# Four late pairs of weight tiles staged in the two output tiles, and the opening written in another order, in a fused attention and feed-forward kernel

## The chip, the cores and the metric

The kernel runs on one core of a Trainium2 chip. The metric is the device time of one execution in microseconds (us), the median of several runs. TensorE (PE) multiplies, VectorE (DVE) and ScalarE (ACT) do the elementwise work, SyncE (SP) issues nearly all DMAs, GpSimd (POOL) only sets constants at the start.

## The reference

Two steps. For each of 8 batches and 8 heads, 512 tokens `x` (64 wide) and 32 states attend to each other in both directions; the results of a batch, 544 rows of 512, then go through a feed-forward network.

```python
scores = scale * np.matmul(x, state.transpose(0, 1, 3, 2))
a = np.exp(scores - scores.max(-1, keepdims=True))
a /= a.sum(-1, keepdims=True) + 1e-09
xread = np.matmul(a, state)                  # the tokens' rows: 512 a batch
scores2 = scale * np.matmul(state, x.transpose(0, 1, 3, 2))
...
sread = np.matmul(a2, x)                     # the states' rows: 32 a batch
...
h = x @ w_in                                 # 512 -> 2048, x now the 4352 rows
g = h * np.clip(h + 3.0, 0.0, 6.0) / 6.0
return (g @ w_out).astype(np.float32)        # 2048 -> 512
```

All of it is float32.

## The kernel before

**Products.** `xread` is never formed: `a @ state @ w_in` is computed as `a` times W' = `state @ w_in`, 256 rows of (head, state) by 2048 for each batch (`wprime`, products at L507, made for a chunk of 512 columns at a time, in the opening for smaller parts). A batch is 16 steps of 128 columns. `first(n)` multiplies `a` by one step of W' into a PSUM bank `ps_h` (there are two); ACT (L998) and DVE (L1000) make `g` of it; `second(n)` multiplies `g` by 128 rows of `w_out` into the four banks `acc0` to `acc3`, two steps later by rank. A float32 product is made of three products of rounded halves (L948): ACT writes the rounded `..._hi` (L305, L410) and DVE the rest `..._lo` (L306, L412). So a step has 6 first and 12 second products of 128x512. Step 0 of batch 0 alone is multiplied plainly (L977, L1017). A ninth pass has the 256 rows of `sread`.

**Attention.** The x of batch 0 is transposed by TensorE (L617), its scores (L682) go through a softmax in seven short DVE and ACT instructions for each quarter (L694 to L705), written into an output tile, and TensorE turns the result out of it (L713) into `a` (copies at L715 and L716). The x of every later batch is loaded in 16 small pieces (L494) into two `raw` tiles, which DVE transposes (four times L607); TensorE makes the scores (L507 on `tmp`). What `sread` needs is transposed by DVE (two times L871) and moved inside the memory by 16 small DMAs (L879); the x for it lies in `xb` (L478). TensorE reads it at L905.

**Weights.** Both matrices come in once. A load (L370) brings a tile of 128 rows, or a pair of such tiles; the words are put together by one ACT cast (L379) and one DVE instruction (L384) for each tile, a "decode" below; a tile of `w_out` is then split in halves (L410, L412). The dict `PLACES` says where a pair is staged: `early0` to `early3` are the rooms in which later halves of `w_out` will live, and the four rooms hold its ten pairs, one after the other. The other tiles of `w_out` go through the three `raw` tiles, which x and the moves of `sread` use as well.

**Output tiles.** The pool `outp` has two tiles, `ot`. One holds the softmax of batch 0 until it is turned; later they hold the results of a batch (`L1041`, `L1044`, stored at L1052) and every third W' chunk.

**What sets the order.** Every operation is put into a plan (`Plan.add`) with its engine, a cost, a rank, what it reads and writes. `Plan.order` makes one sequence: as long as the list `OPENING` lasts, it takes the operation whose number stands there, after that the one that could start first by the costs and ranks. Each engine executes its part of the sequence in order, SP's DMAs among them; a DMA waits in SP's queue until the tile that it fills is free. Between TensorE's operations of the opening, `issue` puts filler products on a constant (`wake`, L1235), as many as the plan's times leave room for.

Of the kernel before, what the change touches and what calls it, by code (L numbers as in the profile page):

```python
# [12 lines left out]
U32 = mybir.dt.uint32  # L13
# [53 lines left out]
class Plan:  # L67
# [33 lines left out]
    def order(self):  # L101
# [19 lines left out]
        channel = 0.0  # L121
        flying = [0.0] * 8
        row, self.start, self.took = [], [0.0] * n_ops, [0.0] * n_ops
        while len(row) < n_ops:
            best = None
            told = opening[len(row)] if len(row) < len(opening) else None
            for e, numbers in open_ops.items():
# [3 lines left out]
                for n in numbers:  # L131
# [6 lines left out]
                    t = max(clock[e], ready[n])  # L138
# [30 lines left out]
            if size:  # L169
                channel = max(channel, t + 0.5) + size / self.transfer  # L170
                done = max(channel, t) + 2.0
                flying.remove(min(flying))
                flying.append(done)
# [33 lines left out]
def tile_state_attention_then_hardswish_ffn(  # L207
# [82 lines left out]
    def Q(rank, size, do, reads=(), writes=(), after=()):  # L290
        return plan.add("Q", 0.49, rank, do, reads, writes, after, size)
# [46 lines left out]
    def weight(kind, k, n, place, rank, load_rank):  # L338
# [8 lines left out]
        def pieces():  # L347
            if place[0] == "raw":
                return get(place, lambda: stage.tile([P, 512, 2], U32, name="raw")).unsqueeze(1)
            c, half = HOMES[int(place[0][-1])]  # L350
            t = get(place, lambda: cpool.tile(
                [P, 2, 512, 2], U32, name=place[0], tag=f"w_out_{half}{c}"))
            return t[:, place[2] : place[2] + n] if n == 1 else t
# [34 lines left out]
        Q(load_rank, {("in", 1): 537.0, ("in", 2): 925.0, ("out", 1): 465.0, ("out", 2): 930.0}[kind, n], load, writes=[key])  # L388
        lo = key + ("lo",)
        wide = 0.08 + 0.54 * n  # L390
        for i in range(n):
            top = ("top", (kind, k + i))
            S_(0.62, rank, lambda i=i: upper(i), [key], [top])
# [31 lines left out]
    wp_at, scores_at = {}, {}  # L425

    def load_state(b, rank, after=()):
# [15 lines left out]
        if b < TURNED:  # L443
            plan.add("Q", 1.35, rank, load, (), [key], after, 400.0)
            return
        plan.add("Q", 1.8, rank, load_blocks, (), [key], after, 400.0)
# [36 lines left out]
    def load_turned(b, rank, after=()):  # L483


        for g in range(NG):
            key = ("raw", ("x", b, g))
            for i in range(2):
                for u in range(2):
                    for k in range(D // NS):  # L490
# [9 lines left out]
                        Q(rank, 65.536, load, writes=[(*key, i, u, k)], after=after)  # L500
# [163 lines left out]
    def tokens_by_rows(after, banks):  # L664
# [9 lines left out]
        for q in range(NQ):  # L674
# [3 lines left out]
            def scores(q=q, ps=ps):  # L678
# [17 lines left out]
            V(0.35, r[1], lambda m1=m1, view=view, bt=bt: nc.vector.tensor_tensor(  # L696
                bt(), view(), wide(m1()), op=ALU.subtract), [m1_key, ps], [part_key])
            S_(0.38, r[2], lambda bt=bt: nc.scalar.activation(bt(), bt(), AF.Exp, scale=SCALE),
# [567 lines left out]
```

## Time and profile before

| | us |
|---|---|
| median of 3 runs | 657.22 (656.95 to 658.18) |
| the profiled execution | 655.46 |
| its span | 653.7 |
| TensorE busy in it | 641.6 |
| granted TensorE clock | 0.999 |
| DMA, moved in it | 46.25 MB |

A line of the table of stretches has the stretch in us from the span's start, its length, then busy us (and instructions) of PE, PE's weight loads, DVE, ACT and POOL, the granted clock, the DMA engines' busy share and GB/s. A line in order of time has start, duration, engine, line, operation, the tile written and the tiles read, and sizes; x2 means two such instructions in a row, and in brackets stands how long the engine had been idle before it and what ended that. `SPq` lines are issues of DMAs; the data lands some us later.

### The profile page before, as it was taken

What the parts mean: (1) busy time and instruction counts of PE and PEld (TensorE: products, weight loads), DVE (VectorE), ACT (ScalarE), POOL (GpSimd) and SP (SyncE); (2) the same over time, 40 slices, a digit from 0 to 9 for tenths busy, and PEclk for the clock granted to TensorE, in tenths of its full rate; (3) what the DMA queues carried; (4) which work ended last, traced back from release to release, by engine and by line L of the source; (5) the groups of instructions that cost most, each with busy time, mean ns of one, the idle gap of its engine ahead of it and who ended that gap; (6) DMA issues with size and microseconds to landing.
All of it is one profiled execution on the core that took longest, in us unless ns stands there. A gap on an engine that the chain in (4) does not pass through costs nothing.

```text
span 653.7 us, 9891 instructions
## 1 busy us (share of the span) xinstructions
PE 641.6 (98%) x3934; PEld 500.3 (77%) x3934; DVE 393.0 (60%) x685; ACT 293.1 (45%) x510; POOL 1.2 (0%) x7
## 2 busy tenths in 40 slices
PE   8999999989999999999999999999999999999997
PEld 6577778767877877787868777787778787788896
DVE  6988785468487356944686356834595344443552
ACT  5988454334344343633344344534344333433542
POOL 0000000000000000000000000000000000000000
PEclk9999999999999999999999999999999999999999
DMA  8985500604840503132131405041131001000101
GB/s 285 339 268 179 117 10 10 118 15 107 120 133 11 86 2 103 33 51 46 64 70 20 78 1 134 1 76 21 66 66 30 3 1 66 0 1 2 64 1 33
DMA packets 135270, 46.25 MB, mean 71 GB/s; under 512 B 123576, under 2 KB 129208, under 8 KB 135096
## 3 DMA queue, kind: packets, MB, share of 16 engines
q1 hardware_dynamic: 135080, 45.36, 28.5%
q8 instruction: 31, 0.51, 0.3%
q10 hardware_dynamic: 144, 0.26, 0.1%
q14 instruction: 15, 0.12, 0.1%
HBM read 33.02 MB, written 8.91 MB: 64 GB/s over the span
## 4 chain that ended last, share of the span: by engine, by line
PE 85%; SPq 4%; DMA 4%; DVE 3%; ACT 2%; issue 1%; DVEq 0%; ACTq 0%
PE acc L948 51%; PE ps_h L948 27%; PE ps_s L507 4%; PE ps_h L507 2%; SPq L879 1%; SPq L494 1%; DMA raw<-in_x_dram 1%; DMA early<-in_moe_w_out_dram 1%; PE ps_h L905 1%; SPq L478 1%; ACT tops L379 1%; DMA early<-in_moe_w_in_dram 1%; DMA raw<-raw 1%; DVE w_in L384 0%; ACT g L998 0%
## 5 line engine op out<-in xcount | busy, mean ns | idle before, releaser
L948 PE MATMUL acc<-w_out_hi,g_hi 128*128 128x512 f32 x540 | 213.4, 395 | 0.1
L948 PE MATMUL acc<-w_out_lo,g_hi 128*128 128x512 f32 x540 | 210.6, 390 | 0.0
L948 PE MATMUL acc<-w_out_hi,g_lo 128*128 128x512 f32 x540 | 210.2, 389 | 0.0
L998 ACT ACTIVATE g<-ps_h,three 128x512 f32<-128x512 f32 (+1 forms) x144 | 95.6, 664 | 221.9 <-PE ps_h L948 210.9
L1000 DVE SCALAR_TENSOR_TENSOR g<-g,ps_h 128x512 f32<-128x512 f32 (+1 forms) x144 | 94.3, 657 | 150.7 <-ACT g L998 149.9
L948 PEld LDWEIGHTS acc<-w_out_hi,g_hi 128*128 128x128 f32 x540 | 101.4, 188 | 34.5 <-issue 12.6
L306 DVE TENSOR_TENSOR g_lo<-g,g_hi 128x512 fp32r<-128x512 f32 (+1 forms) x143 | 93.9, 657 | 49.2 <-ACT g_hi L305 48.0
L305 ACT CAST g_hi<-g 128x512 fp32r<-128x512 f32 (+1 forms) x143 | 85.0, 595 | 85.1 <-DVE g L1000 80.3
L948 PEld LDWEIGHTS acc<-w_out_hi,g_lo 128*128 128x128 f32 x540 | 101.4, 188 | 21.7 <-DVE g_lo L306 0.2
L948 PEld LDWEIGHTS acc<-w_out_lo,g_hi 128*128 128x128 f32 x540 | 101.5, 188 | 19.6
L948 PE MATMUL ps_h<-aT_hi,wp_hi 128*128 128x512 f32 (+1 forms) x246 | 90.4, 367 | 3.3 <-DVE wp_lo L306 2.9
L948 PE MATMUL ps_h<-aT_hi,wp_lo 128*128 128x512 f32 (+1 forms) x246 | 89.1, 362 | 0.4 <-DVE wp_lo L306 0.4
L948 PE MATMUL ps_h<-aT_lo,wp_hi 128*128 128x512 f32 (+1 forms) x246 | 89.1, 362 | 0.0
L948 PEld LDWEIGHTS ps_h<-aT_hi,wp_hi 128*128 128x128 f32 x246 | 46.4, 189 | 13.4 <-issue 3.6
L948 PEld LDWEIGHTS ps_h<-aT_lo,wp_hi 128*128 128x128 f32 x246 | 46.4, 189 | 8.2 <-DVE aT_lo L306 0.5
L948 PEld LDWEIGHTS ps_h<-aT_hi,wp_lo 128*128 128x128 f32 x246 | 46.4, 189 | 7.8 <-DVE wp_lo L306 0.7
L948 PE MATMUL ps_h<-aT_hi,wp 128*128 128x512 f32 x144 | 50.2, 389 | 0.0
L948 PEld LDWEIGHTS ps_h<-aT_hi,wp 128*128 128x128 f32 x144 | 27.0, 188 | 5.7
L607 DVE STREAM_TRANSPOSE tmp<-raw 128x512 f32<-128x512 f32 x28 | 19.1, 699 | 15.9 <-DMA raw<-in_x_dram 12.3
L948 PE MATMUL ps_h<-aT_lo,wp 128*128 128x512 f32 x72 | 28.0, 389 | 0.0
L379 ACT CAST tops<-early 128x512 f16<-128x512 bf16 x25 | 18.2, 779 | 5.0 <-DMA early<-in_moe_w_out_dram 2.8
L507 PE MATMUL ps_s<-w_in,stT 64*32 64x512 f32 (+1 forms) x320 | 19.6, 548 | 0.0
(124 smaller groups left out, 427.4 us busy)
## 6 DMA issues: line engine op xcount, KB each, us to landing
xb<-in_x_dram SPq DMA_DIRECT2D x32, 256.0 KB, 4.2
out_dram<-ot SPq DMA_DIRECT2D x8, 1024.0 KB, 4.4
raw<-in_x_dram SPq DMA_DIRECT2D x112, 64.0 KB, 2.1
early<-in_moe_w_in_dram SPq DMA_DIRECT2D x7, 1023.0 KB, 5.8
early<-in_moe_w_out_dram SPq DMA_DIRECT2D x4, 1023.5 KB, 5.4
raw<-raw SPq DMA_DIRECT2D x112, 32.0 KB, 2.0
raw<-in_moe_w_out_dram SPq DMA_DIRECT2D x7, 511.8 KB, 7.1
early<-in_moe_w_in_dram SPq DMA_DIRECT2D x2, 511.0 KB, 6.4
```

Of the source, the lines that this page charges most:

```text
L305: S_(cost, rank, lambda: nc.scalar.copy(hi(), src()), reads, [writes[0]])
L306: V(cost, rank, lambda: nc.vector.tensor_tensor(lo(), src(), hi().bitcast(F32), op=ALU.subtract), [*reads, writes[0]], [writes[1]])
L379: nc.scalar.copy(out[..., 1], digits(pieces().bitcast(BF16), 2, i))
L478: nc.sync.dma_start(x_tile(b)[:, :, k, :], x_v[b, k])
L494: nc.sync.dma_start(t[rows, i].rearrange("t (a c) -> t a c", c=NS), x[b, 4 * g + 2 * i + u, :, k * NS : (k + 1) * NS].rearrange("(a t) c - ...
L507: nc.tensor.matmul(out[u][cols, :], made["stT", b][rows, cols], moving(q)[rows], start=True, stop=True,)
L607: V(0.7, rank[0], lambda q=q, key=key: nc.vector.transpose(xT(b, q), made[key][:, q % 2]), [(*key, q % 2, u, k) for u in range(2) for k in ...
L879: nc.sync.dma_start(dst[:, :, q], src[:, :, c])
L905: nc.tensor.matmul(bank(pr)[cols, u * D : (u + 1) * D], e2T(b, u)[:, j * P + q * NS : j * P + (q + 1) * NS], x_tile(b)[:, NG * q + u, j, : ...
L948: nc.tensor.matmul(ps, l, r, start=start and k == 0, stop=stop and k == n - 1)
L998: S_(cost + 0.05, rank, lambda: nc.scalar.activation(g(), bank(ps)[:, :width], AF.Relu, bias=three), [ps], [g_key])
L1000: V(cost, rank, lambda: nc.vector.scalar_tensor_tensor(g(), g(), 6.0, bank(ps)[:, :width], op0=ALU.min, op1=ALU.mult), [ps], [g_key])
```

## The change

Four pairs are staged elsewhere: `w_out` 4-5, 6-7 and `w_in` 12-13, 14-15 go into the two output tiles (under the tile name `wide`), two pairs in each, one after the other, in place of `early2` and `early3`. In the plan their loads come after the first multiplications of batch 0's softmax. `OPENING` is written anew and has 675 numbers for 631. Some costs in the plan are other numbers: they have no effect but through the order.

```diff
-5 2 1 0 24 3 4 35 11 80 36 27 6 29 30 28 93 31 32 33 14 49 34 41 25 19 50 51 37 26 52 42 38 39 53 43 57 54 44
+5 0 1 3 11 2 4 33 24 80 34 27 93 29 31 32 6 30 28 37 19 41 38 12 14 57 42 43 35 44 58 39 36 59 45 60 13 49 40
...
-                channel = max(channel, t + 0.5) + size / self.transfer
-                done = max(channel, t) + 2.0
+                channel = max(channel, t + 1.3) + size / self.transfer
+                done = channel + 1.6
...
-    def Q(rank, size, do, reads=(), writes=(), after=()):
-        return plan.add("Q", 0.49, rank, do, reads, writes, after, size)
+    def Q(rank, size, do, reads=(), writes=(), after=(), cost=0.53):
+        return plan.add("Q", cost, rank, do, reads, writes, after, size)
...
+            if place[0] == "ot":
+                return get(place, lambda: outp.tile([P, 2, 512, 2], U32, name="wide", tag="ot"))
...
+          after=first_exps if place[0] == 'ot' else ())
...
-            S_(0.62, rank, lambda i=i: upper(i), [key], [top])
+            S_(0.65, rank, lambda i=i: upper(i), [key], [top])
...
-        plan.add("Q", 1.8, rank, load_blocks, (), [key], after, 400.0)
+        plan.add("Q", 2.6, rank, load_blocks, (), [key], after, 400.0)
...
-            V(0.35, r[1], lambda m1=m1, view=view, bt=bt: nc.vector.tensor_tensor(
+            shifted = V(0.35, r[1], lambda m1=m1, view=view, bt=bt: nc.vector.tensor_tensor(
                 bt(), view(), wide(m1()), op=ALU.subtract), [m1_key, ps], [part_key])
+            first_exps.append(shifted)
...
-        ("in", 4): ("early0", 1), ("in", 6): ("early1", 1), ("out", 4): ("early2", 1),
-        ("out", 6): ("early3", 1), ("in", 8): ("early2", 2), ("in", 10): ("early3", 2),
-        ("out", 8): ("early2", 3), ("out", 10): ("early3", 3), ("in", 12): ("early2", 4),
-        ("in", 14): ("early3", 4),
+        ("in", 4): ("early0", 1), ("in", 6): ("early1", 1), ("out", 4): ("ot", ("w", 0)),
+        ("out", 6): ("ot", ("w", 1)), ("in", 8): ("early2", 2), ("in", 10): ("early3", 2),
+        ("out", 8): ("early2", 3), ("out", 10): ("early3", 3), ("in", 12): ("ot", ("w", 2)),
+        ("in", 14): ("ot", ("w", 3)),
```

The other edits of the diff are costs of the same kind. In the changed kernel the lines stand up to 7 further down. Three places show what the new list moves.

The first is DVE at the end of batch 0's softmax (`ot`, with sums `s`) up to the first `g`; `early` and `raw` rows are decodes, `nm` belongs to the states' softmax. Before:

```order
L384 SCALAR_TENSOR_TENSOR raw<-raw,tops 128x512
L702 TENSOR_SCALAR s_190<-s_190 128x8
L704 RECIPROCAL s_190<-s_190 128x8 x2
L705 TENSOR_TENSOR ot<-ot,s_190 128x8x32 x2
L781 TENSOR_REDUCE nm_297<-ps_s 128x2
L384 SCALAR_TENSOR_TENSOR w_in_179<-early_142,tops 128x4x128 x2
L716 COPY w_in_314<-acc_308 128x512
L781 TENSOR_REDUCE nm_297<-ps_s 128x2
L306 TENSOR_TENSOR wp_lo<-acc_253,wp_hi 128x128
```

and now:

```order
L711 TENSOR_TENSOR ot<-ot,s_190 128x8x32 x2
L307 TENSOR_TENSOR wp_lo<-acc_275,wp_hi 128x128
L387 SCALAR_TENSOR_TENSOR w_in_240<-early_137,tops 128x4x128
L307 TENSOR_TENSOR wp_lo<-acc_274,wp_hi 128x128
L722 COPY w_in_309<-acc_304 128x512
L387 SCALAR_TENSOR_TENSOR w_in_240<-early_137,tops 128x4x128
L307 TENSOR_TENSOR aT_lo<-w_in_309,aT_hi 128x512 x2
L387 SCALAR_TENSOR_TENSOR raw<-raw,tops 128x512
L787 TENSOR_REDUCE nm_346<-ps_s 128x2
L1006 SCALAR_TENSOR_TENSOR g<-g,ps_h 128x512
```

Both `wp_lo` stand ahead of the copy of `a`, one decode fewer stands ahead of the last multiplications, and the first reduction for the states stands behind `aT_lo`.

The second is SP's queue of loads from about 30 us on (the pieces `raw<-in_x_dram` are x of batch 1). Before:

```order
L370 DMA early_444<-in_moe_w_out_dram 128x2x2047
L370 DMA raw<-in_moe_w_out_dram 128x2047
L370 DMA early_497<-in_moe_w_out_dram 128x2x2047
L440 DMA st_raw<-in_state_dram 32x4x32 x4
L370 DMA raw<-in_moe_w_out_dram 128x2047
L370 DMA early_562<-in_moe_w_in_dram 128x4x1023
L370 DMA early_595<-in_moe_w_in_dram 128x4x1023
L370 DMA early_641<-in_moe_w_out_dram 128x2x2047
L370 DMA early_683<-in_moe_w_out_dram 128x2x2047
L494 DMA raw<-in_x_dram 32x16x32 x16
```

and now, from the load of `w_in` 6-7 on:

```order
L373 DMA early_327<-in_moe_w_in_dram 128x4x1023
L373 DMA wide<-in_moe_w_out_dram 128x2x2047 x2
L373 DMA early_429<-in_moe_w_in_dram 128x4x1023
L499 DMA raw<-in_x_dram 32x16x32
L373 DMA early_496<-in_moe_w_out_dram 128x2x2047
L499 DMA raw<-in_x_dram 32x16x32 x7
L373 DMA raw<-in_moe_w_out_dram 128x2047
L499 DMA raw<-in_x_dram 32x16x32 x3
L373 DMA wide<-in_moe_w_in_dram 128x4x1023
L445 DMA st_raw<-in_state_dram 32x4x32 x4
L499 DMA raw<-in_x_dram 32x16x32 x2
L373 DMA early_646<-in_moe_w_out_dram 128x2x2047
```

After these come one piece of x, the last `wide` pair (`w_in` 14-15), the last two pieces and the last three tiles of `w_out`. The two `w_out` pairs have moved ahead of `w_in` 10-11, and x of batch 1 lies between the weights.

The third is DVE ahead of the scores of batch 2 (the rows `tmp<-raw` transpose its x). Before:

```order
L306 TENSOR_TENSOR wp_lo<-ps_s,wp_hi 128x512
L306 TENSOR_TENSOR wp_lo<-ps_h,wp_hi 128x512
L1000 SCALAR_TENSOR_TENSOR g<-g,ps_h 128x512
L306 TENSOR_TENSOR g_lo<-g,g_hi 128x512
L306 TENSOR_TENSOR wp_lo<-ps_s,wp_hi 128x512
L1000 SCALAR_TENSOR_TENSOR g<-g,ps_h 128x512
L607 STREAM_TRANSPOSE tmp<-raw 128x512 x2
L306 TENSOR_TENSOR wp_lo<-ps_h,wp_hi 128x512
L306 TENSOR_TENSOR g_lo<-g,g_hi 128x512
```

and now:

```order
L307 TENSOR_TENSOR wp_lo<-ps_h,wp_hi 128x512
L307 TENSOR_TENSOR g_lo<-g,g_hi 128x512
L307 TENSOR_TENSOR wp_lo<-ps_s,wp_hi 128x512
L307 TENSOR_TENSOR wp_lo<-ps_h,wp_hi 128x512
L307 TENSOR_TENSOR wp_lo<-ps_s,wp_hi 128x512
L1006 SCALAR_TENSOR_TENSOR g<-g,ps_h 128x512
L456 STREAM_TRANSPOSE stT<-st_raw 128x128
L1006 SCALAR_TENSOR_TENSOR g<-g,ps_h 128x512
L307 TENSOR_TENSOR g_lo<-g,g_hi 128x512
L612 STREAM_TRANSPOSE tmp<-raw 128x512 x4
```

All four `wp_lo` (the last W' products of batch 1) now stand ahead of the four transposes.

More of the change, by code (lines that the diff above doesn't have):

```diff
@@ L386, in join @@
             )
-        Q(load_rank, {("in", 1): 537.0, ("in", 2): 925.0, ("out", 1): 465.0, ("out", 2): 930.0}[kind, n], load, writes=[key])
+        Q(load_rank, {("in", 1): 537.0, ("in", 2): 960.0, ("out", 1): 465.0, ("out", 2): 1000.0}[kind, n], load, writes=[key],
+          after=first_exps if place[0] == 'ot' else ())
         lo = key + ("lo",)
@@ L425, in tile_state_attention_then_hardswish_ffn @@
     wp_at, scores_at = {}, {}
+    first_exps = []
     def load_state(b, rank, after=()):
@@ L443, in load_state @@
         if b < TURNED:
-            plan.add("Q", 1.35, rank, load, (), [key], after, 400.0)
+            plan.add("Q", 1.39, rank, load, (), [key], after, 400.0)
             return
-        plan.add("Q", 1.8, rank, load_blocks, (), [key], after, 400.0)
+        plan.add("Q", 2.6, rank, load_blocks, (), [key], after, 400.0)
     def turn_state(b, rank, after):
@@ L499, in load @@
                             )
-                        Q(rank, 65.536, load, writes=[(*key, i, u, k)], after=after)
+                        Q(rank, 65.536, load, writes=[(*key, i, u, k)], after=after, cost=0.62)
     def all_heads(b, out, moving):
@@ L795, in exps @@
                                              accum_out=r2()[:, NG + NG * i + u : NG + NG * i + u + 1])
-                    S_(0.6, rank(5), exps, [ps[i], n_key], [("tmp", ("e2", b, u), i), (*r_key, u, i)])
+                    S_(0.48, rank(5), exps, [ps[i], n_key], [("tmp", ("e2", b, u), i), (*r_key, u, i)])
             V(0.08, rank(6), lambda: nc.vector.scalar_tensor_tensor(
@@ L865, in move @@
                             nc.sync.dma_start(dst[:, :, q], src[:, :, c])
-                        Q(rank, 16.384, move, [blocks_key], [e2T_key(b, g, c, q)])
+                        Q(rank, 16.384, move, [blocks_key], [e2T_key(b, g, c, q)], cost=0.65)
             return
@@ L879, in move @@
                     nc.sync.dma_start(dst[:, :, q], src[:, :, c])
-                Q(rank, 32.768, move, [(*blocks_key, g) for g in range(NG)], [e2T_key(b, 0, c, q)])
+                Q(rank, 32.768, move, [(*blocks_key, g) for g in range(NG)], [e2T_key(b, 0, c, q)], cost=0.65)
     def put(c, ps, cols):
```

45 rows, old and new, of the table OPENING are left out of this document.

## The prediction

> **What bounds the kernel now.** I read the page's busy shares first, then the table of stretches (busy us of each engine, its instructions, granted clock, DMA share, GB/s), then TensorE's own order of time, looking for starts further apart than the work between them. The last line is from the chain of waits: the twelve second products of one step take 2.72, so one product 0.227 and the six first ones of a step 1.36.
>
> ```profile
> PE 641.6 (98%) x3934; PEld 500.3 (77%) x3934; DVE 393.0 (60%) x685; ACT 293.1 (45%) x510; POOL 1.2 (0%) x7
> 0.00:20.00 20.00, 16.49 (x166) 12.38 (x166) 13.51 (x39) 13.28 (x27) 1.17 (x7) 1.00 0.88 304
> 20.00:60.00 40.00, 39.20 (x235) 25.32 (x234) 34.83 (x63) 35.12 (x67) 0.00 (x0) 1.00 0.84 285
> 60.00:120.00 60.00, 60.00 (x377) 45.47 (x376) 43.32 (x76) 31.01 (x53) 0.00 (x0) 1.00 0.24 45
> 120.00:140.00 20.00, 17.08 (x147) 13.02 (x145) 10.05 (x16) 5.10 (x8) 0.00 (x0) 1.00 0.47 86
> 200.00:600.00 400.00, 400.00 (x2340) 314.83 (x2340) 224.06 (x369) 161.01 (x269) 0.00 (x0) 1.00 0.20 42
> ...
> 204.52 2.72 PE acc L948 x12
> ```
>
> TensorE ends the kernel. From 200 to 600 us it is busy for 400.00 of 400.00, so nothing is to be had there. What an order can win lies before 200: the time until the first real product, and the places where TensorE waits. In 20 to 60 ACT and DVE are busy for 35 of 40 us each: there the covers are thin.
>
> ```profile
> 132.13 0.39 PE L948 MATMUL acc<-w_out_lo,g_hi 128*128 128x512 f32 x1
> 132.35 0.39 PE L948 MATMUL acc<-w_out_hi,g_lo 128*128 128x512 f32 x1
> 135.66 0.47 PE L948 MATMUL ps_h<-aT_hi,wp_hi 128*128 128x512 f32 x1 [2.92 <-DVE wp_lo L306]
> 132.91 0.71 DVE L607 STREAM_TRANSPOSE tmp<-raw 128x512 f32<-128x512 f32 x1 [2.74 <-DMA raw<-in_x_dram]
> 134.23 0.71 DVE L607 STREAM_TRANSPOSE tmp<-raw 128x512 f32<-128x512 f32 x1 [0.61 <-DMA raw<-in_x_dram]
> 134.86 0.65 DVE L306 TENSOR_TENSOR wp_lo<-ps_h,wp_hi 128x512 fp32r<-128x512 f32 x1
> ```
>
> The largest wait: a product starts 0.23 us after its neighbour (132.13, 132.35), and the next one 3.31 after that. TensorE wants wp_lo; DVE has it behind two transposes of batch 2's x, and these wait for x. The wait is made by DVE's order: the transposes aren't needed until the scores of batch 2, at 138.
>
> **The change part by part.**
>
> ```profile
> 168.35 0.39 PE L948 MATMUL acc<-w_out_lo,g_hi 128*128 128x512 f32 x1
> ```
>
> It adds no product, cast, decode or byte. It takes 8 of 43 fillers out of the opening, and from this row on (the last 2,477 of TensorE's) the sequence on every engine is the old one. So the gain is what TensorE has won by this row, and what it waits less behind it.
>
> *Opening, to the second products of step 0* (L1017, now L1023).
>
> ```profile
> 16.83 0.74 DVE L705 TENSOR_TENSOR ot<-ot,s 128x256 f32<-128x256 f32 x2
> 17.63 1.09 PE L713 MATMUL acc<-ident,ot 128*128 128x128 f32 x8 [0.56 <-DVE ot L705]
> 18.56 1.15 PE L1235 MATMUL ps_h<-wake 128*128 128x256 bf16 x9
> 19.29 0.68 DVE L716 COPY w_in<-acc 128x512 f32<-128x512 f32 x1
> 19.54 1.88 PE L977 MATMUL ps_h<-w_in,tmp 128*128 128x512 f32 x4
> 22.37 0.50 PE L948 MATMUL ps_h<-aT_hi,wp_lo 128*128 128x512 f32 x1 [0.37 <-DVE wp_lo L306]
> 22.83 0.68 DVE L1000 SCALAR_TENSOR_TENSOR g<-g,ps_h 128x512 f32<-128x512 f32 x1
> 23.57 2.07 PE L1017 MATMUL acc<-raw,g 128*128 128x512 f32 x4
> ```
>
> DVE's softmax of batch 0 had four weight decodes (0.68) in it and has three. A full decode is 0.6 at DVE's pace (two take 1.28); I count 0.4, since the first score arrives a little later. The last multiply then ends at 17.15 for 17.57. TensorE's turn follows: 1.09, plus 0.2 to its reader, 18.45. DVE has wp_lo, a decode and wp_lo in that pause (1.2), then in a row, as the new order has them: the copy, a decode, two aT_lo, a decode, one reduction, the multiply that makes g: six by 0.6 and 0.68, to 22.75. TensorE has 5 fillers for 9 after the turn (9 took 0.98, so 0.44 less); step 0 then starts near 18.75, and step 1 is through by 22.2, as both wp_lo are early now and the wait at 22.37 goes. The second products so wait for g, and start at 22.8 for 23.57: **-0.8**. Bounds: +0.3, if none of the decode's time is won and g comes later still; -1.4, if they start as soon as TensorE is free at 22.2.
>
> [...]
>
> *Late weight pairs in the output tiles.*
>
> ```profile
> 30.52 0.37 SPq L370 DMA_DIRECT2D early<-in_moe_w_out_dram  x1
> 34.65 0.37 SPq L370 DMA_DIRECT2D early<-in_moe_w_out_dram  x1
> 37.48 1.43 ACT L379 CAST tops<-early 128x512 f16<-128x512 bf16 x2 [2.04 <-DMA early<-in_moe_w_out_dram]
> 44.03 0.39 PE L948 MATMUL acc<-w_out_hi,g_lo 128*128 128x512 f32 x1
> 44.82 0.50 PE L948 MATMUL ps_h<-aT_hi,wp_hi 128*128 128x512 f32 x1 [0.40 <-DVE g L1000]
> ```
>
> The pairs w_out 4-5 and 6-7 were asked for at 30.52 and 34.65, when the early tiles came free; ACT stood 2.04 for the first, DVE's multiply came late behind it, and TensorE lost 0.79 - 0.23 = 0.56. Now one output tile is free from the start and the other after the turn (18.45), so both loads are issued near 20, behind three w_in pairs.
>
> ```profile
> 10.00:20.00 10.00, 8.80 (x119) 6.57 (x119) 9.93 (x31) 8.99 (x19) 0.00 (x0) 1.00 1.04 390
> ```
>
> In the first 20 us DMA moves 304 x 20 = 6.1 MB. The loads ahead of these five pairs are 5.3 MB; of the pairs' 5.2 MB 0.8 are then in too, and 4.4 take 11.3 us at 390 GB/s: the last is in near 32. ACT has 23 entries between the aT_hi casts (done near 20) and its first cast of a wide tile, 0.52 each (35.12 in 67): near 32 too, when w_out 4-5 has been in for 2.7, and the next two casts follow six entries later. So ACT's wait goes: **-0.6**. Bounds: 0 (ACT and DVE are full there) and -0.6.
>
> *x of batch 1 earlier.*
>
> ```profile
> 65.04 8.29 SPq L494 DMA_DIRECT2D raw<-in_x_dram  x16
> 76.16 2.12 PE L507 MATMUL ps_s<-tmp,stT 64*32 64x512 f32 x16
> 76.45 0.71 DVE L607 STREAM_TRANSPOSE tmp<-raw 128x512 f32<-128x512 f32 x1 [1.55 <-DMA raw<-in_x_dram]
> 138.01 1.09 PE L507 MATMUL ps_s<-tmp,stT 64*32 64x512 f32 x16
> ```
>
> The scores of batch 1 take 2.12 where those of batch 2 take 1.09: they wait for the last transpose. SP's 16 issues of x now stand between the weights, 14 of them ahead of the last w_in pair. That pair waits for the lo half of w_out 6-7, 47 DVE entries behind the g of step 0 (22.75); at 40 us for 63 entries this is near 52, so x is in by 56. TensorE reaches the scores near 68: from 22.8 on 4.0 for step 0's second products, ten steps of first products (1.36), eight of second ones (2.72), six W' sets and the turn of e2 with their switches (6). **-1.0**, bounds 0 and -1.0.
>
> *x of batch 2 behind wp_lo.*
>
> ```profile
> 107.48 0.69 DVE L871 STREAM_TRANSPOSE raw<-tmp 128x512 f32<-128x512 f32 x1
> 108.23 0.76 SPq L879 DMA_DIRECT2D raw<-raw  x1
> 109.19 2.15 SPq L440 DMA_DIRECT2D st_raw<-in_state_dram  x4
> 131.98 0.60 SPq L494 DMA_DIRECT2D raw<-in_x_dram  x1
> ```
>
> All four wp_lo now precede the four transposes, so the 3.31 - 0.23 go: **-3.1**. What is late next? The moves (L879) can't start before the second L871, and with x and xb the queue needs 23.75 us from 108.23 to its last issue; DVE is through with x at 134.9, 26.7 after 108.23. The four state loads (2.15) now go ahead of the moves, so I take 24.5. From the second L871 (L877) to the scores TensorE has seven steps of first products, 6.25 of second ones and two W' sets: 9.5 + 17.0 + 2.1 = 28.6. So x is transposed some 3 us before the scores. Behind the transposes DVE has the multiply g of step 24, needed only after the scores: covered by 2.2 us of scores and reading. Bounds: -3.1, and -0.5 if the queue runs as slowly as in 146 to 176, when 16 moves and 16 pieces shared it with an output store.
>
> *Behind 168.4.*
>
> ```profile
> 179.46 0.39 PE L948 MATMUL acc<-w_out_hi,g_lo 128*128 128x512 f32 x1
> 179.97 0.50 PE L948 MATMUL acc<-w_out_hi,g_hi 128*128 128x512 f32 x1
> ```
>
> 0.51 - 0.23: 0.28 lost, as DVE stood for batch 3's x. Its pieces are issued with the earlier moves now: **-0.3**, bounds 0 and -0.3.
>
> *At nothing*: plan numbers that reach no row behind 168.4; the tile name, which changes no byte; out of batch 0 still stored behind the moves, before batch 1 wants its tile. Without that cover the output multiplies would wait for the store.
>
> *New small waits*: the row order cannot show them, the trace of before does not have them. The old order, written by the same kind of plan, left 0.56 and 0.28 besides its two large ones; I give the new one **+1.0**, bounds 0 and +3 (one wait like the largest).
>
> Sum: -0.8 - 0.6 - 1.0 - 3.1 - 0.3 + 1.0 = -4.8. The profiled execution took 655.46 (span 653.7): 650.7. The median of the runs is 657.22, 1.8 above it; the forecast for the median is **652.4**.
>
> **The rivals.**
>
> *All goes and nothing new comes*: -5.8, with a faster opening -6.4: about 651. For: every term has its own row. Against: DVE and ACT full in 20 to 60.
>
> *x of batch 2 is late still*: the wait moves from wp_lo to the scores. For: 36 issues in one queue, each near 0.6. Against: 3 us of cover. At the term's bound, 2.6 less gain: 655.0.
>
> [...]
>
> *Nothing won*: DVE and ACT are the bound from 20 to 100, and early loads only wait in their tiles; the large wait is paid in several small ones. 657.2. Against: DVE idles for 17 of 60 us in 60 to 120.
>
> *Slower*: two pairs in one tile. w_in 14-15 cannot be asked for before w_out 6-7 has left the output tile (near 52, above), and W' of chunk 3 wants it near 64, 4 before the scores. From issue to decode an early pair took 37.48 - 30.52 + 1.9, near 9 us; so 3 us of cover. It decides once that pair is over 3 us late; 8 us late costs 5, and as all steps of chunk 3 queue behind it on an ACT that is full, 2 more: 657.22 - 4.8 + 7 = 659.4. For: x pieces now lie among these loads. Against: DMA is 0.73 to 0.77 busy in 40 to 60, as this shows.
>
> ```profile
> 40.00:50.00 10.00, 9.60 (x59) 7.08 (x58) 8.37 (x13) 9.01 (x16) 0.00 (x0) 1.00 0.77 238
> 50.00:60.00 10.00, 9.97 (x67) 6.38 (x67) 8.18 (x15) 8.76 (x16) 0.00 (x0) 1.00 0.73 257
> ```
>
> **How the numbers follow.** Forecast 0.49 (651.3 to 653.8), all goes 0.11, x late 0.18, cold array 0.03, nothing won 0.09, slower 0.10. A measurement of this kernel can tell 0.2%, 1.3 us, from no change. Faster by more (under 655.9): 0.49 + 0.11 + 0.18 + 0.03 = 0.81; same 0.09; slower 0.10. The range that leaves out 2 in 10 runs from 650.6 to 655.7.
>
> **What would show it.** In the changed kernel: L983 starts near 18.8 and L1023 near 22.8; no ACT cast of a wide tile waits for a DMA; the scores of batch 1 last 1.1; no wait for wp_lo over 0.5 us; the scores of batch 2 start near 130; TensorE is 5 us earlier at the row that was at 168.4. The prediction is wrong if a wait of over 2 us stands anywhere between 20 and 168, or if the opening is no earlier.

## The result, and the profile after

| us | before | after |
|---|---|---|
| median, runs | 657.64 (4) | **648.87** (4: 648.32 to 649.16) |
| the profiled execution, its span | 655.46, 653.7 | 649.16, 647.3 |
| TensorE busy in it | 641.6 | 639.0 |

The ratio is 0.9868 (95% interval 0.9851 to 0.9885): 1.3% faster, below the forecast's 652.4 and below the low end of its range, 650.6. The two profiled executions lie 6.3 apart, the two medians 8.8: this difference is the first thing to be explained.

From the changed kernel's page, its busy shares:

```profile
PE 639.0 (99%) x3926; PEld 500.9 (77%) x3926; DVE 393.3 (61%) x685; ACT 292.4 (45%) x510; POOL 1.2 (0%) x7
```

Its table of stretches, with the columns as before:

```profile
20.00:60.00 40.00, 39.27 (x232) 27.88 (x231) 35.58 (x63) 32.92 (x62) 0.00 (x0) 1.00 0.96 290
60.00:120.00 60.00, 59.58 (x389) 44.58 (x388) 45.09 (x77) 33.38 (x58) 0.00 (x0) 1.00 0.26 59
120.00:140.00 20.00, 20.00 (x161) 15.76 (x160) 14.45 (x28) 7.79 (x14) 0.00 (x0) 1.00 0.26 34
200.00:600.00 400.00, 400.00 (x2346) 315.05 (x2346) 220.29 (x364) 160.41 (x268) 0.00 (x0) 1.00 0.20 42
```

From 120 to 140 us TensorE is busy throughout, where it was for 17.08. From 200 to 600 it is busy for 400.00 of 400.00, as before. Its order of time on TensorE at the places that the prediction named:

```profile
16.75 1.09 PE L719 MATMUL acc<-ident,ot 128*128 128x128 f32 x8 [0.22 <-DVE ot L711]
18.22 1.88 PE L983 MATMUL ps_h<-w_in,tmp 128*128 128x512 f32 x4
22.22 3.87 PE L1023 MATMUL acc<-raw,g 128*128 128x512 f32 x8 [0.73 <-DVE g L1006]
61.34 0.39 PE L954 MATMUL acc<-w_out_hi,g_lo 128*128 128x512 f32 x1
62.15 0.50 PE L954 MATMUL ps_h<-aT_hi,wp_hi 128*128 128x512 f32 x1 [0.42 <-DVE g L1006]
68.41 1.09 PE L512 MATMUL ps_s<-tmp,stT 64*32 64x512 f32 x16
128.71 1.09 PE L512 MATMUL ps_s<-tmp,stT 64*32 64x512 f32 x16
177.40 1.09 PE L512 MATMUL ps_s<-tmp,stT 64*32 64x512 f32 x16
```

The row of the kernel before that stands at the place of the last one:

```profile
183.75 1.09 PE L507 MATMUL ps_s<-tmp,stT 64*32 64x512 f32 x16
```

The second products of step 0 start 1.35 earlier (22.22 for 23.57). The scores of batch 1 last 1.09, for 2.12. Those of batch 2 start at 128.71 with nothing waiting. One new wait is there: 62.15 - 61.34 - 0.23 = 0.58. At the scores of batch 3, where TensorE's order is the old one again, it is 6.35 earlier, and the spans differ by 6.4: all that this pair of executions shows was won before.

### The profile page after: what moved, and what is told of

It reads as the page before. It is cut to its first block, busy times and chain, and to the rows that moved or that the text cites. A ratio compares the mean times of both kernels' runs of the same rounds, so it can differ in the third digit from the quotient of the medians.

```text
span 647.3 us, 9869 instructions
## 1 busy us (share of the span) xinstructions
PE 639.0 (99%) x3926; PEld 500.9 (77%) x3926; DVE 393.3 (61%) x685; ACT 292.4 (45%) x510; POOL 1.2 (0%) x7
## 4 chain that ended last, share of the span: by engine, by line
PE 92%; DVE 3%; DMA 2%; ACT 1%; SPq 1%; issue 0%
PE acc L954 55%; PE ps_h L954 28%; PE ps_s L512 4%; PE ps_h L512 2%; DMA wide<-in_moe_w_in_dram 1%; PE ps_h L911 1%; SPq L499 1%; PE acc L1023 1%; DVE w_in L387 1%; PE ps_h L1241 1%; DVE g L1006 1%; DMA raw<-in_x_dram 0%; DVE m L699 0%; ACT tops L382 0%; DVE g_lo L307 0%
## 5 line engine op out<-in xcount | busy, mean ns | idle before, releaser
L307 DVE TENSOR_TENSOR wp_lo<-ps_h,wp_hi 128x512 fp32r<-128x512 f32 x18 | 11.8, 687 | 11.0 <-ACT wp_hi L306 10.9
```

Of the source, the lines that this page charges most:

```text
L307: V(cost, rank, lambda: nc.vector.tensor_tensor(lo(), src(), hi().bitcast(F32), op=ALU.subtract), [*reads, writes[0]], [writes[1]])
```

## The experiments

In these kernels the list is written out to its end (2,200 numbers), so that single entries can be moved; lines then stand up to 67 further down. Ratios are to the kernel before on the same chip, whose medians were 656.75, 657.13, 656.54 and 657.67 in the four sets (rows 1 to 4, 5 to 8, 9 to 12, 13 and 14).

| kernel | median | executions | ratio, 95% interval |
|---|---|---|---|
| before_again | 656.95 | 12 | 1.0000 (0.9989 to 1.0012) |
| x2_behind | 654.25 | 6 | 0.9956 (0.9939 to 0.9972) |
| opening_only | 658.68 | 12 | 1.0035 (1.0019 to 1.0052) |
| staging_only | 655.37 | 12 | 0.9976 (0.9962 to 0.9990) |
| keep_awake | 655.06 | 12 | 0.9973 (0.9959 to 0.9987) |
| wp_lo_last | 651.12 | 4 | 0.9914 (0.9898 to 0.9931) |
| first_30 | 660.02 | 9 | 1.0057 (1.0036 to 1.0078) |
| first_70 | 661.44 | 6 | 1.0072 (1.0057 to 1.0087) |
| after_again | 648.40 | 6 | 0.9873 (0.9852 to 0.9895) |
| two_moves | 648.87 | 6 | 0.9881 (0.9859 to 0.9903) |
| nine_fillers | 648.89 | 4 | 0.9883 (0.9858 to 0.9908) |
| order_only | 683.16 | 4 | 1.0400 (1.0373 to 1.0428) |
| relu_ahead | 648.39 | 4 | 0.9865 (0.9845 to 0.9885) |
| g_ahead | 648.82 | 5 | 0.9869 (0.9849 to 0.9889) |

**before_again**: the kernel before, unchanged.

> The kernel before, unchanged, run again to see how its executions spread. In the first set its profiled execution had a span of 653.7 us and its other runs came out near 657.6, while the changed kernel's profiled execution lies 0.3 us from its median. Theory A: something in this kernel varies from execution to execution by some 2 us (its waits for x, which hang on when transfers land, are the candidates), so spans spread from 653.7 to 656 and a profile with a longer span shows a longer wait near 76 or near 132 us. Theory B: the profiled execution was one lucky value; spans all lie near 655.9 and the same waits are there in a new profile with a span of 655.5 to 656. Theory C: the clock differs; then spans differ and no wait does.

The waits are the same ones, and still its profiled execution has a span of 656.1, 2.4 more than the first. TensorE's order of time behind the large wait:

```profile
133.27 0.39 PE L948 MATMUL acc<-w_out_hi,g_lo 128*128 128x512 f32 x1
136.53 0.73 PE L948 MATMUL ps_h<-aT_hi,wp_hi 128*128 128x512 f32 x1 [2.87 <-DVE wp_lo L306]
137.06 0.63 PE L948 MATMUL ps_h<-aT_lo,wp_hi 128*128 128x512 f32 x1
137.49 0.63 PE L948 MATMUL ps_h<-aT_hi,wp_lo 128*128 128x512 f32 x1
...
140.46 1.09 PE L507 MATMUL ps_s<-tmp,stT 64*32 64x512 f32 x16
```

The stretches around it; the column ahead of the last two is the granted clock:

```profile
134.00:136.00 2.00, 0.00 (x0) 0.00 (x0) 1.37 (x3) 0.00 (x0) 0.00 (x0) 1.00 0.20 33
136.00:138.00 2.00, 1.47 (x4) 1.21 (x5) 1.57 (x3) 0.39 (x1) 0.00 (x0) 0.64 0.00 0
138.00:140.00 2.00, 2.00 (x6) 1.56 (x5) 0.00 (x0) 0.46 (x2) 0.00 (x0) 0.50 0.00 0
140.00:142.00 2.00, 2.00 (x55) 0.85 (x57) 1.29 (x2) 0.46 (x1) 0.00 (x0) 1.00 0.01 4
```

Products behind the wait start 0.43 apart where they start 0.23 apart in the first profile: half clock, 0.50 in the stretches. From the waiting product to the scores it takes 140.46 - 136.53 = 3.93, for 138.01 - 135.66 = 2.35 in the first: 1.58 more. The other 0.8 lies ahead of it: the waiting product itself starts 0.87 later. So the wait of 3 us has a second price, and the first profiled execution had been spared it. Of 82 executions of this kernel 59 have a mean clock of 0.997 or less and a mean span of 655.5; 23 have 0.999 or 1.000 and 653.9. Theory A had the size and the place right but not the cause: theory C's clock differs, and keep_awake shows that the idle time of the wait brings it down.

**keep_awake**: in `first`, ahead of the products of the step that waits:

```diff
+            if n == 26:
+                for _ in range(24):
+                    nc.tensor.matmul(bank(("ps_s", ("C", 2, 0)))[:, :256], wake[:, :P], wake, start=True, stop=True)
             ah, al = (made["aT", b][h]() for h in ("hi", "lo"))
```

> The kernel before with 24 more filler products (2.6 us of them) in the place where TensorE waits for 3 us near 132; they write a score bank that is free there and is overwritten by the scores. They do nothing for the wait itself. My theory, formed on the new profile of the kernel before: after that wait TensorE mostly runs at half clock for 3.42 us (136.57 to 139.99), which costs 1.7 us, and the first profiled execution escaped it. With fillers the clock stays at 1.00, the wait stays at 3.0, and the median falls by some 1.3 us, to 655.4 (ratio 0.998), with spans of 653 to 655. Rival: the lower clock costs nothing, because DVE is late behind the wait anyway, or the fillers delay the waiting product: 0 or slower.

TensorE's rows at the wait:

```profile
132.83 2.79 PE L982 MATMUL ps_s<-wake 128*128 128x256 bf16 x24
136.14 0.47 PE L948 MATMUL ps_h<-aT_hi,wp_hi 128*128 128x512 f32 x1 [0.52 <-DVE wp_lo L306]
136.45 0.40 PE L948 MATMUL ps_h<-aT_lo,wp_hi 128*128 128x512 f32 x1
```

The waiting product is as late as before (3.31 behind the fillers' start), and the time falls by 2.1 (ratio 0.9973): all 12 executions have a clock of 0.998 or more. Useless work in the gap makes the kernel faster. This shows the cause of the second price; the first estimate of 1.3 lies within the interval. The mean span is 653.3, 0.6 under that of the executions that had been spared; what brings these 0.6 stays open.

**x2_behind**: the kernel before with two entries moved.

```diff
-607 521 567 600 520 577 606 601 568
+607 567 600 577 521 520 606 601 568
```

> The kernel before with two instructions moved and nothing else: the two transposes of batch 2's x that DVE has ahead of the last wp_lo stand right behind it. My theory: the 3.08 us that TensorE waits near 132 is made by DVE's order; it goes, and about 0.2 us comes back at the scores of batch 2, since the last transpose would end near 134.9: -2.9 us, ratio 0.9956. Rival: x lands too late for the scores as well, and the wait only moves to them: -0.5 us or less.

The ratio is the expected one, but by another sum. In TensorE's order of time a wait is left:

```profile
135.41 0.49 PE L1015 MATMUL acc<-w_out_hi,g_lo 128*128 128x512 f32 x1 [1.08 <-DVE g_lo L373]
```

and in DVE's stands why:

```profile
132.87 0.71 DVE L674 STREAM_TRANSPOSE tmp<-raw 128x512 f32<-128x512 f32 x1 [2.32 <-DMA raw<-in_x_dram]
134.07 0.71 DVE L674 STREAM_TRANSPOSE tmp<-raw 128x512 f32<-128x512 f32 x1 [0.49 <-DMA raw<-in_x_dram]
134.71 0.65 DVE L373 TENSOR_TENSOR g_lo<-g,g_hi 128x512 fp32r<-128x512 f32 x1
```

The transposes wait for x as before, and now a `g_lo` behind them makes TensorE wait: 1.24 above the pitch, and 0.37 in the change of tiles behind it. So these two moves take 3.08 - 1.61 = 1.5 off the wait. The rest of the 2.5 is the half clock, which this wait of 1.2 did not bring: all 6 executions have 0.998 or more. The changed kernel has that `g_lo` ahead of the transposes as well; how much its whole order on DVE would win with x as late as here was not run.

**wp_lo_last**: the changed kernel with the last `wp_lo` behind the transposes (step 23's first products give way by three entries, as the bank comes free later).

```diff
-579 498 577 555 497 581 495 564 500 556 557 572
+579 498 555 497 581 495 500 556 557 564 572
...
-567 522 571
+567 522 577 571
```

> The changed kernel with one instruction moved back: the last wp_lo of batch 1 stands behind all four transposes of batch 2's x, as it stood behind the last two of them before. Theory of the prediction: the wait is made by DVE's order, so putting it back makes TensorE wait again: 2 us or more slower than the changed kernel. Theory now: the wait needed late x as well (x has landed at 124.9 in the changed kernel, and the bank that this wp_lo holds is wanted only near 128.5); within 0.4 us of the changed kernel, 649 us.

TensorE's largest wait between 100 and 200 us:

```profile
122.55 0.50 PE L1020 MATMUL ps_h<-aT_hi,wp 128*128 128x512 f32 x1 [1.50 <-DVE g L1072]
```

Slower than the changed kernel by 2.3 to 2.7 (its medians are 648.87 and, in after_again, 648.40), as the theory of the prediction had it, but not by its path: there is no wait for `wp_lo`. It holds one of the two `ps_h` banks, so the first products of two steps, as I read the order, must share the other, and the second of them waits 1.66 above the pitch for `g`. My theory of 0.4 fell with it.

**staging_only**: the changed kernel's tiles and costs with the whole old list.

```diff
-5 0 1 3 11 2 4 33 24 80 34 27 93 29 31 32
+5 2 1 0 24 3 4 35 11 80 36 27 6 29 30 28
```

> The changed kernel's tiles and planning numbers with the whole order of the kernel before (and 44 fillers, not 35): the late pairs are staged in the output tiles, but asked for where they were asked for before. My theory: the tiles alone bring nothing, as the loads stand behind the same queue entries: within 0.3 us of before, the wait near 44 stays at 0.56 us. Rival: the loads start when their tile is free, and the early tiles were what held them: then the 2.04 us that ACT waited at 37.5 go and TensorE wins 0.5 us.

From SP's queue, the first two loads into output tiles:

```profile
26.60 0.63 SPq L439 DMA_DIRECT2D wide<-in_moe_w_out_dram  x1
28.33 0.44 SPq L439 DMA_DIRECT2D wide<-in_moe_w_out_dram  x1
```

My theory fell, and the rival holds with more than the 0.5 that it gave: 1.4 faster. In the same queue order the two `w_out` pairs are asked for 3.9 and 6.3 earlier than before (30.52, 34.65), since SP no longer stands waiting for the early tiles. The wait at 44 is gone; the wait of 3 us and the half clock stay (a mean clock of 0.997 or less in 9 of 12).

**opening_only**, **first_30**, **first_70**: the changed list's first 117, 143 and 326 numbers, then the others in the old order.

> The changed kernel's order for the first 117 entries of the plan (through the second products of step 0, with the fewer fillers, and the late pairs in the output tiles), then the order of the kernel before for all that is left. My theory: the opening's gain is passed on whole, -1.35 us (second products of step 0 at 22.2 us), and the waits near 44, 76 and 132 stay at 0.6, 1.0 and 3.1: span 652.3, ratio 0.998. Rival: the waits behind it are set by transfers at fixed times, so they grow by what the opening won: 0 to -0.4 us.

> The changed kernel's order for the first 143 entries of the plan (through the second products of step 1 and the W' behind them), then the order of the kernel before. Theory: the opening's 1.35 and the 0.5 at 44 are won, and the waits near 76 and 132 stay, with the half clock behind the second: 655.0, ratio 0.997. Rival, as the cut at 117 entries showed: where the two orders are joined, ACT's and SP's lists no longer fit, and TensorE waits 2 us or more near 26 to 40: 657 or slower.

> The changed kernel's order for the first 326 entries of the plan (through the scores of batch 1 and the step behind them, near 72 us), then the order of the kernel before. Theory: won are the opening (1.35), the waits near 44 and 54 (0.76) and that at the scores of batch 1 (1.03), lost the new one near 61 (0.58): -2.6; the wait near 132 stays at 3 us with the half clock behind it: 654.2, ratio 0.996. Rival: the chain of batch 1 ends earlier too, so x of batch 2 lands earlier, and the wait near 132 shrinks with it: 650 to 651.5.

All three are slower than both whole orders. Two rows of TensorE from opening_only:

```profile
28.57 0.50 PE L1020 MATMUL ps_h<-aT_hi,wp_hi 128*128 128x512 f32 x1 [1.89 <-ACT wp_hi L372]
39.31 0.51 PE L1020 MATMUL acc<-w_out_hi,g_hi 128*128 128x512 f32 x1 [1.75 <-ACT w_out_hi L480]
```

A row of TensorE from first_70:

```profile
79.01 0.80 PE L1020 MATMUL acc<-w_out_hi,g_lo 128*128 128x512 f32 x1 [4.45 <-DVE g_lo L373]
```

and the row of ACT that it comes from:

```profile
74.86 0.76 ACT L448 CAST tops<-raw 128x512 f16<-128x512 bf16 x1 [4.71 <-DMA raw<-in_moe_w_out_dram]
```

The waits stand behind the seam: after it the old list casts a tile that the new one had asked for late. As tests of additivity the cuts failed; only first_30's rival had foreseen it. Two things they do show: ahead of its seam first_70 reaches the scores of batch 1 at 67.68 with no new wait, and all three have the wait near 136 (2.6 to 3.3 above the pitch) with a lower clock behind it: the stretches of opening_only from 140 to 142 and of first_70 from 140 to 144 have 0.50, and in first_30 a product at 141.11 takes 0.59, for 0.39. What the changed order wins ahead of 70 does not by itself take that wait away. The theory and the rival of opening_only and of first_70 all fell.

**after_again**, **nine_fillers**: the changed kernel, and the same with four more fillers.

```diff
-else int((gap - 0.25) / 0.13)):
+else int((gap - 0.25) / 0.13) + (4 if n == until else 0)):
```

> The changed kernel, unchanged, beside the kernel before on one chip and with more executions than the first set's four. What it has to tell: whether the 8.8 us of the first set are the change or partly the spread of the kernel before. From the runs so far: executions of the kernel before at a clock of 0.999 or 1.000 have spans near 654.1, those at 0.997 and less near 655.4; the changed kernel's are near 647.0. Theory: the changed kernel stays at 648.9 with a small spread (no wait of 2 us or more before its last product, so no half clock that costs anything), and the difference of medians is 8.0: ratio 0.988. Rival: 8.8 or more, 0.9866.

> The changed kernel with 9 fillers after the turn, as before, for its 5. Theory of the prediction: the opening gains 0.44 by the shorter row of fillers, so this gives it back: +0.4. Theory now: second products of step 0 wait for g, which DVE makes behind a decode and a maximum whatever TensorE did; they start at most 0.15 later relative to the turn's end, and the time stays within 0.3 us of the changed kernel.

TensorE's rows of the turn, of the second products of step 0 and of the scores of batch 1 in after_again:

```profile
17.74 1.09 PE L719 MATMUL acc<-ident,ot 128*128 128x128 f32 x8 [0.22 <-DVE ot L711]
23.22 3.87 PE L1023 MATMUL acc<-raw,g 128*128 128x512 f32 x8 [0.72 <-DVE g L1006]
68.69 1.09 PE L512 MATMUL ps_s<-tmp,stT 64*32 64x512 f32 x16
```

The first two of these in nine_fillers:

```profile
17.38 1.09 PE L719 MATMUL acc<-ident,ot 128*128 128x128 f32 x8 [0.22 <-DVE ot L711]
22.86 3.87 PE L1023 MATMUL acc<-raw,g 128*128 128x512 f32 x8 [0.31 <-DVE g L1006]
```

From the turn to the second products it takes 5.48 with 5 fillers and 5.48 with 9: the fillers cost nothing, `g` sets it. (The plan's costs do have an effect besides the order: they set the fillers, 35 now for 43.) And two executions of one kernel start these products 1.00 apart (22.22, 23.22), while the scores follow 0.28 apart: in the first, the wait near 62 takes most of the opening's lead back. The changed kernel's spans lie from 646.4 to 647.5 in 10 executions, mean 646.8. after_again's median is 8.1 below the kernel before, as its theory had it; the interval of its ratio holds the rival's 0.9866 too.

**two_moves**, **relu_ahead**, **g_ahead**: single entries of the changed list.

```diff
-98 7 114 153 15 170 8 116 109 131 9 110 20 132
+98 7 114 153 109 15 170 116 110 8 9 131 20 132
+98 7 114 153 109 15 170 116 131 110 8 20 9 132
...
-338 283 286 339 273 307 140 290 284
+338 283 286 339 290 273 307 140 284
```

relu_ahead has the last line alone, two_moves the first new line and the last, g_ahead the second and the last.

> The changed kernel with two places of its order mended, for the two waits that its trace shows. First: the Relu and the multiply that make g of step 0 stand ahead of a weight cast on ACT, and ahead of a weight decode and a maximum on DVE; TensorE waited 0.73 for this g. Second: ACT's Relu of step 9 stands ahead of the cast of w_in 15, which waited 1.96 for its load; TensorE waited 0.58 there. Theory: second products of step 0 start 0.8 earlier and the wait near 62 goes: -1.3 us, 647.5, if the decode and the maximum that are 0.7 later have cover. Rival: the decode that is moved back feeds the weights of steps 1 and 2, and the wait comes back at 26 to 30: within 0.4 us of the changed kernel.

> The changed kernel with ACT's Relu of step 9 ahead of its cast of w_in 15, and nothing else. If the load of w_in 14-15 sets the stretch to 68 us by way of this Relu, then the wait near 62 (0.58 in one profile of the changed kernel, none in another that opened 1.0 later) cannot come, the scores of batch 1 start 45.3 us after the second products of step 0 in every execution, and the mean falls by 0 to 0.6 with the opening: 648.2. If g of step 0 alone counts, nothing changes: 648.5 and the same spread.

> The same, and g of step 0 is made earlier: its Relu stands ahead of one weight cast, its multiply ahead of one weight decode; the maximum that two_moves had pushed back stays where the changed kernel has it, so that the softmax of the early scores, for which W' waited 0.97 at 26 in two_moves, is not late. Theory: second products of step 0 start 3.4 to 3.5 after step 0's first product instead of 4.0, nothing waits at 26 or 62, and the time falls by 0.5 to 0.9: 647.8 (ratio to the changed kernel 0.999). Rival: another wait takes the place again before 68, as in two_moves: 648.5 or more.

ACT's rows near 60 in the changed kernel:

```profile
60.05 0.78 ACT L382 CAST tops<-wide 128x512 f16<-128x512 bf16 x1 [1.96 <-DMA wide<-in_moe_w_in_dram]
60.70 0.68 ACT L1004 ACTIVATE g<-ps_h,three 128x512 f32<-128x512 f32 x1
```

ACT's cast in after_again:

```profile
60.04 0.78 ACT L382 CAST tops<-wide 128x512 f16<-128x512 bf16 x1 [0.95 <-DMA wide<-in_moe_w_in_dram]
```

TensorE's two rows of relu_ahead that its expectation names:

```profile
22.23 3.87 PE L1089 MATMUL acc<-raw,g 128*128 128x512 f32 x8 [0.73 <-DVE g L1072]
67.69 1.09 PE L578 MATMUL ps_s<-tmp,stT 64*32 64x512 f32 x16
```

and one of g_ahead:

```profile
26.04 0.66 PE L578 MATMUL ps_s<-w_in,stT 64*32 64x256 f32 x14 [0.36 <-ACT tmp L866]
```

Both executions start the cast near 60.04 though they opened 1.00 apart: it waits for the load of `w_in` 14-15, and the Relu stands behind it. But the load sets no fixed time. Three other profiles with the same order up to there (nine_fillers, wp_lo_last, first_70) start this cast at 58.94 to 59.24 and have no wait of TensorE near 62. These are the rows of first_70, whose second products start at 22.22 as in the changed kernel's first profile:

```profile
59.24 0.77 ACT L448 CAST tops<-wide 128x512 f16<-128x512 bf16 x1 [1.15 <-DMA wide<-in_moe_w_in_dram]
67.68 1.09 PE L578 MATMUL ps_s<-tmp,stT 64*32 64x512 f32 x16
```

With the Relu ahead, the scores follow 45.46 after the second products (45.3 expected; 46.19 in the changed kernel's first profile). This does not test the edit: the load was in time in that execution (the cast starts at 58.57 and waits for nothing), and after_again, nine_fillers, wp_lo_last and first_70 have 45.45 to 45.47 without it. g_ahead starts the second products 3.40 after step 0's first, and two_moves 3.39, as expected, for 4.00; but both then lose 0.97 at W' near 26, which waits for ACT's exponentials of the early scores, so that their rivals hold. In time none of the three can be told from the changed kernel: no faster version was found.

**order_only**: the new order, as near as the old `PLACES` allow.

> The changed kernel's order of rows with the tiles of the kernel before: the four late pairs are staged in the early tiles again, and each step stands where the changed kernel has it, or behind it as soon as its tile allows (246 of 2200 entries give way to one that stood behind them). Theory: the order rests on w_out 4-5 and 6-7 being asked for near 20 us; without the output tiles they come after the early tiles are free, casts and decodes of late pairs hold ACT and DVE up, and most of the gain is lost: 654 or slower. Rival: the order alone does it: within 1 us of the changed kernel, 650.

TensorE's longest wait:

```profile
66.27 1.11 PE L574 MATMUL ps_s<-w_in,stT 64*32 64x256 f32 x16 [10.47 <-DVE w_in L451]
```

As the theory had it, slower than 654, and 27 us slower than before: one wait alone, for the late `w_in` tiles, is 10.5. The new order cannot do without the tiles; the tiles do something without the order.

## Why the prediction missed

**From the profile to the median.** This is the step that failed. "The median of the runs is 657.22, 1.8 above it" was added to the changed kernel as if it were a constant; in the changed kernel the profiled execution lies 0.3 above the median (649.16, 648.87). Most of the 1.8 was the half clock behind the wait at 132, which left with that wait: in the kernel before, 59 of 82 executions have the lower mean clock, at 1.6 each, 1.15 in the mean. (For the three runs behind 657.22 no clock is on record; the other 0.6 is put down to the spread.) What let the term through is that one execution, with 1.00 across the 3.08 us at 132, was taken for all. The 1.00 that the table gives for the first 20 us misleads too: the trace's first entry for the clock begins at 4.23, and where there is none the table prints 1.00. The 15 fillers ahead of it start 0.21 apart, those behind it 0.11, so TensorE began at half the pace. That moves no term: in the changed kernel the entry begins at 6.75, and the second products of step 0 still start 1.35 earlier.

Of the miss of 3.5 this term is 1.8, the way from the changed kernel's profile to its median 0.3, and the sum below 1.5. Without the 1.8 the forecast would have been 650.7, still 1.8 above the measured median.

The 0.03 for a cold array was meant for a pause in the changed opening that slows its first steps; no run shows that: step 0's products take 1.88 in both kernels. What the runs showed in its place is the half clock behind the wait near 132, which the change removes: in before_again it lasts 3.41 (136.57 to 139.98) and adds 1.58 from the waiting product to the scores.

**The sum**, by the two profiled executions:

| step | forecast | measured |
|---|---|---|
| opening to second products of step 0 | -0.8 | -1.35 |
| late weight pairs: waits at 44 and 54 | -0.6 | -0.56, -0.20 |
| x of batch 1 | -1.0 | -1.03 |
| x of batch 2 | -3.1 | -3.08 |
| behind 168 | -0.3 | -0.28 |
| new small waits | +1.0 | +0.58 |
| product behind a wait: in these two traces the next one follows after 0.31 to 0.34, not 0.23; four such waits went, one came | not counted | -0.30 |
| rest, not traced | not counted | -0.13 |
| sum | -4.8 | -6.35 |

- *Opening.* Right in the mean; the -1.35 is this pair's. In seven profiles with the new opening the second products start at 22.49 in the mean, in five with the old one at 23.22: -0.7. Of this the turn is 0.31 earlier (16.96 for 17.27, where I counted 0.4; in this pair DVE's last multiply ends 0.87 earlier, 16.70 for 17.57). The other 0.42 come between the turn and the second products, which wait for `g`, as the prediction said; four fillers more or fewer do not move them (nine_fillers).
- *Late pairs.* The wait at 44 went, as forecast, and one at 54 that I had not counted. "No ACT cast of a wide tile waits for a DMA" was wrong: a cast of `w_in` 14-15 waited 1.96 here, and 0.22 to 1.15 in four other profiles. This is the rival with two pairs in one tile, where it said, its pair asked for at 51.60 ("near 52"); its price is 0.58 in this profile and nothing in those four, not 7.
- *x of batch 1.* As forecast.
- *x of batch 2.* Right in size. "The wait is made by DVE's order" was half of it: two moves in that order take 1.5 of 3.08 (x2_behind), and one `wp_lo` put back behind the transposes does not bring the wait again (wp_lo_last). The other half is that x is there, which I had counted as cover only. The moves begin at 99.34, for 108.23, and the last of the 16 pieces is asked for by 122.6, for 132.6; the four state loads stand behind them (122.89), not ahead as I read it. The transposes then end 1.3 before the scores, not 3:

```profile
99.34 4.05 SPq L885 DMA_DIRECT2D raw<-raw  x6
124.93 2.49 DVE L612 STREAM_TRANSPOSE tmp<-raw 128x512 f32<-128x512 f32 x4 [0.33 <-DMA raw<-in_x_dram]
```

- *Behind 168.* Right in size. But the row at 168.35 is followed by the old sequence on TensorE and ACT only (2,868 of TensorE's products in the trace, counting that row, not 2,477): DVE transposes batch 3's x earlier in its order up to 180, and SP's queue differs up to 186.
- *New waits.* The +1.0 came from what the old order had left; the new one left 0.58 in one profile and nothing in four.

In executions of the kernel before that the half clock spared, the mean span is 653.9, and the changed kernel's is 646.8: 7.1. Of these the pair of profiles shows 6.4, as the changed kernel's profiled execution is one of its longest. With 1.15 for the half clock the difference is 8.2; the first set's 8.8 has 0.6 of the spread of the kernel before in it.

## What to carry to other kernels

One profiled execution is one draw: before its time is set against a median, look at the spread of spans and clocks over all executions, above all where TensorE waits as long as here: behind its 3.08 us another 1.6 was lost in 59 of 82 executions and not in the others, and that part went with the wait. An order and the tiles that make it possible are one thing: tiles alone brought 1.4 of 8, the order without them lost 27, and every seam between two good orders was worse than either. What is won early can be lost at the next instruction that stands in its engine's order behind a load, as in one of five profiles here; find that load before adding up gains ahead of it.

## What the runs showed of the hardware

The wait of TensorE for some 3 us in the kernel before came with half clock in 59 of 82 executions, by their mean clock of 0.997 or less, and not in the others, with the same instructions and nearly the same wait. In the first profile TensorE was idle for 2.92 ahead of the waiting product, and every stretch from 126 to 148 has a clock of 1.00. In before_again it was idle for 2.87, and from 136.57 to 139.98 the clock was 0.50. Half clock stands behind the same wait in staging_only (3.06 idle, 0.50 in the stretch from 136 to 138) and in opening_only (2.40 idle, 0.50 from 140 to 142). Longer waits elsewhere had it too: behind the 4.45 of first_70 products start 0.43 apart from 79.60 to 84.30, behind the 10.47 of order_only from 67.89 to 69.60. What decides in which executions of the kernel before it comes was not shown.

The waits of 1.2 in x2_behind (1.08 idle) and of 1.7 in wp_lo_last (1.50 idle) came without it: by the mean clock, 0.998 or more, none of 6 and 4 executions lost clock there. Products on a constant, 24 in a pause of 3.3, kept it away in 12 of 12 executions of keep_awake (0.998 or more).

A mean clock under 1.00 cost nothing in the changed kernel's profile: its 0.998 comes from the time behind the last product (which starts at 642.17), as its last two stretches show, with 0.93 and 0.50.

```profile
643.30:645.30 2.00, 0.00 (x0) 0.00 (x0) 0.00 (x0) 0.00 (x0) 0.00 (x0) 0.93 0.68 193
645.30:647.30 2.00, 0.00 (x0) 0.00 (x0) 0.00 (x0) 0.00 (x0) 0.00 (x0) 0.50 0.19 70
```
